# Copying the first batch's state five steps later in the first 256-token block of a fused retention and gated feed-forward kernel

## The chip, the cores and the metric

The kernel runs on one core of one Trainium2 chip. The metric is the device time of one execution in microseconds (us), taken as the median of several runs. Time before: 303.86 us, the median of three runs (303.48 to 303.89).

The engines are named as in the profile: PE is TensorE (matrix products), DVE is VectorE, ACT is ScalarE, POOL is GpSimd, and SP is the engine whose queue issues nearly all transfers.

## The reference

Retention (attention with a decay per head) on 8 batches, 8 heads, 576 positions and 64 elements per head, and then a gated feed-forward network on the 4608 tokens with 512 features and 1536 hidden units:

```python
scores = scale * np.matmul(q, k.transpose(0, 1, 3, 2))
gamma = 1.0 - 2.0 ** (-5.0 - np.arange(H))
rel = pos[:, None] - pos[None, :]
Dmat = np.where(rel >= 0, gamma[:, None, None] ** rel[None], 0.0)
attn = np.matmul(scores * Dmat[None], v)
x = attn.transpose(0, 2, 1, 3).reshape(B * S, H * D)
gate = 1.0 / (1.0 + np.exp(-(x @ w_gate)))
out = (gate * (x @ w_val)) @ w_out
```

## The kernel before

The positions of a batch are cut into chunks of 128 (the last one has 64). Inside a chunk the products of queries and keys are masked and multiplied with the values; what lies in earlier chunks enters through a running **state** per batch and head, a 64 x 64 matrix that sums key-by-value products. A last chunk of 64 positions needs the state after the fourth chunk.

The tokens pass in blocks: 512 tokens first, then the blocks of `BLOCKS`: two of 256 tokens (`w` = 0 and 1) and seven of 512. The first 512 tokens include the first batch's four whole chunks. That is why the first batch's state after its fourth chunk is already there, in the tile `sbd[3]`, before block 0 begins. `sbd[3]` holds it in block-diagonal form (two heads on each 128 x 128 square). The first batch's last chunk is handled much later, as step `(0, LAST)`, and it reads the state from a tile `sf` of the ordinary form. `first_batch_state()` (L833 to L840) makes that tile. It issues two copies on DVE for the halves that stay on their partitions, and two transfers from on-chip memory to on-chip memory on SP's queue for the halves that change partitions.

All instructions are in an order written out by hand. Each engine works through its own list in that order and waits on semaphores; nothing is rescheduled. In block `w` the generator `ffn_units` yields after each unit of PE work, and the list `SUMS_AT` says what is issued behind which unit: `0.3:w10v` means "in block 0, behind unit 3, issue weight sum number 0 of the value weights, group 1, on DVE" (the last letter is v for DVE, p for POOL; it has no effect for the letters c, t and f). The letters are: c `casts_to` (load, scale and cast the next chunks, mostly POOL and SP), f `first_batch_state`, g and w `w_sums` (sums of gate and value weights, L365), t `turn_step` (PE transposes a chunk, and ACT and DVE copy it out, L632), o `wo_sums` (L324).

The units of a 256-token block come from `h_units` (L876 to L891). Even units are the gate products of two hidden slices (PE `h_g`, then a sigmoid on ACT, L888); odd units are the value products (PE `h_v`, then the gate-times-value product on DVE, L890, with `gv` as output). The accumulators of the units turn through a ring of three PSUM banks, `ffn_psum`:

```python
ps = ffn_psum.tile([P, 2, n], FP32, tag="ffn", name=f"h_{what}_{t0}_{fc}")
...
if what == "g":
    nc.scalar.activation(out=both, in_=ps, func=AF.Sigmoid)
else:
    nc.vector.tensor_tensor(out=both, in0=both, in1=ps, op=ALU.mult)
```

Unit n + 3 takes the bank of unit n. Unit 4 (`h_g` of slices 4 and 5) may start when the DVE product of unit 1 has read its bank. Unit 9 is the value unit of slices 8 and 9, and unit 10 (`h_g` of slices 10 and 11) takes the bank of unit 7, so it waits for unit 7's DVE product. In the text a value unit's DVE product has its unit's number: "product 1" is L890 behind unit 1.

In block 0 the list reads: behind unit 0 the casts up to chunk step 3 and, before the change, the first batch's state; behind unit 3 three weight sums (`g20p` on POOL, `w10v` and `w11v` on DVE); behind unit 6 the turn of chunk step 1 (`t01p`); behind unit 7 `o10p`; behind unit 8 and 9 more; behind unit 10 the scores of two chunk steps (PE `row` and `new`).

Of the kernel before, what the change touches and what calls it, by code (L numbers as in the profile page):

```python
# [16 lines left out]
def kernel(  # L17
# [1477 lines left out]
    def op_first(fcs, nbs, opps):  # L1495
        for fc in fcs:
            for nb in nbs:
# [49 lines left out]
    store(opps[3], 3 * P, on_act)  # L1547
    casts_to(1)

    SUMS_AT = ("0.0:c03p 0.0:f00p 0.3:g20p 0.3:w10v 0.3:w11v 0.6:t01p 0.7:o10p 0.8:c02v "  # L1550
# [4 lines left out]
    sums_at = {}  # L1555
    for x in SUMS_AT:
        at, x = x.split(":")
# [87 lines left out]
```

## Time and profile before

| what | before |
|---|---|
| median of three runs | 303.86 us |
| the profiled execution: its time | 303.85 us |
| its span in the trace | 302.0 us |
| PE busy | 295.0 us (98%) |
| DVE busy | 228.5 us (76%) |
| POOL busy | 222.8 us (74%) |
| ACT busy | 204.5 us (68%) |
| granted PE clock | full in all 40 slices |

The span runs from the first to the last recorded instruction; 1.85 us of the profiled execution's time lie outside of it. A row of the timeline has the start in us, the duration in us, the engine, the line, the operation, output and inputs, and how many instructions were merged; in brackets stands the idle time of the engine before it, and what ended that. Start times count from the start of the span. PE's matrix products are pipelined, so a row's duration reaches into the next row.

### The profile page before, as it was taken

Reading aid. Unit: us, or ns where it says so; the run is one execution under the profiler, and the core shown is the slowest. Engines: PE = TensorE matmul, PEld = TensorE weight load, DVE = VectorE, ACT = ScalarE, POOL = GpSimd, SP = SyncE. Lnnn points to the kernel's source line nnn. Section 1 sums busy time; section 2 is a strip of 40 time slices with the busy share of each in tenths; the row PEclk is TensorE's granted clock in tenths of the full one; section 3 lists DMA queues with packets and bytes.
Section 4 is the critical chain, followed back from the end, with each engine's and each line's share of the span. In section 5 each row is a group of like instructions: output and inputs, shape, how many; then the busy total and the mean of one; then the engine's idle time right before and its main releaser. Section 6 shows DMA issues by size and latency. Waiting matters only on the chain.

```text
span 302.0 us, 10687 instructions
## 1 busy us (share of the span) xinstructions
PE 295.0 (98%) x4430; PEld 249.8 (83%) x4437; DVE 228.5 (76%) x433; ACT 204.5 (68%) x413; POOL 222.8 (74%) x250
## 2 busy tenths in 40 slices
PE   7999999999999999999999999999999999999994
PEld 3687786878868888888888888888888888888883
DVE  6968666875887998789748974896489948945893
ACT  6765464335359747985798589857985698559830
POOL 5675545936569888978997899689978946860780
PEclk9999999999999999999999999999999999999999
DMA  7999999998989989998649967966694154004013
GB/s 200 339 365 401 346 311 245 233 144 186 188 177 212 247 161 209 218 203 243 143 106 207 249 144 156 239 166 141 116 203 141 37 148 168 4 2 140 3 35 104
DMA packets 146464, 54.99 MB, mean 182 GB/s; under 512 B 124400, under 2 KB 139760, under 8 KB 146416
## 3 DMA queue, kind: packets, MB, share of 16 engines
q1 hardware_dynamic: 145328, 53.59, 74.3%
q10 hardware_dynamic: 1088, 0.72, 0.8%
q8 instruction: 34, 0.56, 0.7%
q14 instruction: 14, 0.11, 0.1%
HBM read 37.75 MB, written 9.44 MB: 156 GB/s over the span
## 4 chain that ended last, share of the span: by engine, by line
PE 94%; SPq 2%; DMA 2%; DVE 1%; issue 0%; POOL 0%
PE gatea L1015 12%; PE wa L1015 12%; PE qa L1142 11%; PE qe L1142 9%; PE gatee L1015 6%; PE we L1015 6%; PE h_g L885 4%; PE op L1275 3%; PE op L1502 3%; PE h_v L885 3%; PE gateg L1015 3%; PE wg L1015 3%; PE hg L1343 3%; PE hv L1343 3%; SPq L186 2%; PE val L717 2%
## 5 line engine op out<-in xcount | busy, mean ns | idle before, releaser
L1015 PEld LDWEIGHTS <-wg_sb 128*128 128x128 bf16 x336 | 32.9, 98 | 4.0
L1042 POOL TENSOR_TENSOR gv<-gv,wu 128x512 bf16<-128x512 bf16 x20 | 23.4, 1172 | 15.8 <-DVE wu L1054 15.7
L1142 PEld LDWEIGHTS <-gsum 128*128 128x128 bf16 x312 | 29.9, 98 | 3.7
L429 POOL TENSOR_TENSOR qk<-q,qtab 128x512 bf16<-128x512 f32 x28 | 30.2, 1079 | 3.4 <-DMA q<-in_q_dram 3.4
L1015 PEld LDWEIGHTS <-wv_sb 128*128 128x128 bf16 x296 | 28.9, 98 | 3.4
L1054 DVE TENSOR_TENSOR gu<-gatee,gu 128x512 f32<-128x512 f32 x21 | 14.5, 691 | 19.1 <-ACT gateg L1046 10.1
L942 POOL TENSOR_TENSOR gsum<-gsum,gv 128x256 bf16<-128x256 bf16 (+1 forms) x20 | 17.6, 890 | 14.4 <-DVE gsum L942 12.6
L1015 PEld LDWEIGHTS <-wgt_sb 128*128 128x128 bf16 x252 | 24.6, 98 | 2.9
L1015 PE MATMUL gatea<-xsum,wg_sb 128*128 128x256 bf16 x168 | 25.0, 273 | 0.0
L1142 PEld LDWEIGHTS <-gv 128*128 128x128 bf16 x228 | 21.8, 98 | 2.7
L942 POOL TENSOR_TENSOR gsum<-gv,gsum 128x256 bf16<-128x256 bf16 (+1 forms) x24 | 21.9, 920 | 0.2
L703 DVE TENSOR_TENSOR pt<-row,tri 128x512 bf16<-128x512 f32 x30 | 19.3, 682 | 3.4 <-PE row L686 3.0
L1057 DVE TENSOR_TENSOR gs<-gatea,gs 128x512 f32<-128x512 f32 x21 | 14.5, 689 | 9.3 <-PE gatea L1015 9.2
L429 POOL TENSOR_TENSOR qk<-k,ktab 128x512 bf16<-128x512 f32 x11 | 11.5, 1042 | 13.5 <-DMA k<-in_k_dram 6.2
L442 POOL TENSOR_TENSOR v<-v,ktab 128x512 bf16<-128x512 f32 x19 | 20.9, 1100 | 0.0
L1015 PE MATMUL wa<-xsum,wv_sb 128*128 128x256 bf16 x136 | 20.4, 273 | 0.0
L658 ACT CAST sb<-s 128x512 bf16<-128x512 f32 (+1 forms) x26 | 14.4, 568 | 8.3 <-DVE s L828 8.2
L787 ACT CAST xT<-val 128x512 bf16<-128x512 f32 x26 | 14.7, 592 | 6.8 <-PE val L733 6.8
L942 DVE TENSOR_TENSOR gsum<-gv 128x512 bf16<-128x512 bf16 (+1 forms) x34 | 18.7, 577 | 0.0
L1015 PEld LDWEIGHTS <-wvt 128*128 128x128 bf16 x168 | 16.4, 98 | 1.9
L942 POOL TENSOR_TENSOR gsum<-gv 128x256 bf16<-128x256 bf16 (+1 forms) x20 | 17.5, 879 | 0.0
L1042 POOL TENSOR_TENSOR gv<-gv,ws 128x512 bf16<-128x512 bf16 x14 | 16.3, 1162 | 1.0 <-DVE ws L1057 1.0
(203 smaller groups left out, 878.2 us busy)
## 6 DMA issues: line engine op xcount, KB each, us to landing
k<-in_k_dram SPq DMA_DIRECT2D x26, 256.0 KB, 3.9
q<-in_q_dram SPq DMA_DIRECT2D x26, 256.0 KB, 4.3
v<-in_v_dram SPq DMA_DIRECT2D x26, 256.0 KB, 4.5
out_dram<-ob SPq DMA_DIRECT2D x24, 256.0 KB, 3.3
wg<-in_moe_w_gate_dram SPq DMA_DIRECT2D x12, 256.0 KB, 5.3
wv<-in_moe_w_val_dram SPq DMA_DIRECT2D x12, 256.0 KB, 5.2
wo<-in_moe_w_out_dram SPq DMA_DIRECT2D x12, 256.0 KB, 5.1
v32p<-in_v_dram SPq DMA_DIRECT2D x6, 256.0 KB, 4.8
```

The costliest lines, as they stand in the source:

```text
L429: eng.tensor_tensor(out=to, in0=by_halves(loaded[s][1 - i]), in1=tab, op=ALU.mult)
L442: nc.gpsimd.tensor_tensor(out=natural["v", s], in0=loaded[s][2], in1=tab, op=ALU.mult)
L703: nc.vector.tensor_tensor(out=t[:, y, 0:n].rearrange("p i m t -> p (i m) t"), in0=rows_tile[ss[0]][y][:, 0:n].rearrange("p i m t -> p (i m ...
L787: nc.scalar.copy(out=to, in_=src)
L885: nc.tensor.matmul(ps[:, i], lhsT=w_sb[:, kc, (fc + i) * P:(fc + i + 1) * P], rhs=xT(kc, slice(t0, t0 + n)), start=(kc == 0), stop=(kc == ...
L942: eng.tensor_tensor(out=to, in0=a, in1=b, op=op)
L1015: nc.tensor.matmul(ps[:, f], lhsT=w[:, kc, f * P:(f + 1) * P], rhs=x[:, kc], start=(first and f == 0 and kc == 0), stop=(f == 1 and kc == ...
L1042: eng.tensor_tensor(out=to, in0=to, in1=src[:, part], op=ALU.mult)
L1054: nc.vector.tensor_tensor(out=me["u2"], in0=e, in1=me["u2"], op=ALU.add)
L1057: nc.vector.tensor_tensor(out=me["s5"], in0=a, in1=me["s5"], op=ALU.add)
L1142: nc.tensor.matmul(ps[:, b], lhsT=left(fp)[:, b * P:(b + 1) * P], rhs=right(fp), start=(first and fp == 0 and b == 0), stop=(fp == NFC // ...
L1343: nc.tensor.matmul(ps[:, cols], lhsT=(wg_sb if what == "g" else wv_sb)[:, kc, fc * P:(fc + 1) * P], rhs=xT(kc, cols), start=(kc == 0), sto ...
```

## The change

One entry of `SUMS_AT` gets another place: `first_batch_state()` is issued behind unit 5 of block 0 and no longer behind unit 0. What it issues stays the same.

```diff
-    SUMS_AT = ("0.0:c03p 0.0:f00p 0.3:g20p 0.3:w10v 0.3:w11v 0.6:t01p 0.7:o10p 0.8:c02v "
+    SUMS_AT = ("0.0:c03p 0.5:f00p 0.3:g20p 0.3:w10v 0.3:w11v 0.6:t01p 0.7:o10p 0.8:c02v "
```

In DVE's list the two copies stood ahead of products 1 and 3, the two weight sums and product 5; now they stand behind these five, and ahead of the copy of the turned chunk (L632) and product 7. In SP's list the two transfers keep their place, between the transposing transfers of chunk steps 3 and 4. The lists of PE, ACT and POOL keep their order.

## The prediction

> **What bounds the kernel now.** I read the page's busy shares and its chain first, then the list of what PE waited for, then the chain in order of time around the edit, and last the timeline of each engine there.
>
> ```profile
> PE 295.0 (98%) x4430; PEld 249.8 (83%) x4437; DVE 228.5 (76%) x433; ACT 204.5 (68%) x413; POOL 222.8 (74%) x250
> PE 94%; SPq 2%; DMA 2%; DVE 1%; issue 0%; POOL 0%
> ```
>
> PE is the bound: 94% of the chain that ended last is PE work. A change of DVE's order counts only where PE waits. PE's waits over the whole span are few:
>
> ```profile
> PE idle L242 <- DVE blank L229: 1.1, 1, 1.1
> PE qkp L485 <- ACT qT L476: 0.6, 2, 0.4
> PE h_g L885 <- DVE gv L890: 0.5, 1, 0.5
> ```
>
> The third lies at the edit. The chain in order of time (start, us, what) shows the copies in it:
>
> ```profile
> 53.15 0.89 PE h_g L885 x8
> 54.03 0.63 DVE sf L838
> ...
> 54.70 0.70 DVE gv L890
> 55.40 0.04 issue
> 55.44 1.03 PE h_g L885 x8
> ```
>
> Unit 4 (the `h_g` at 55.44) needs product 1, which stands on DVE behind the copies. Here are the rows of PE, then DVE, then POOL, and the copies apart (min/median/max in ns).
>
> ```profile
> 52.11 1.04 PE L885 MATMUL h_v<-xT,wv_sb 128*128 128x256 bf16 x8
> ...
> 53.85 1.04 PE L885 MATMUL h_v<-xT,wv_sb 128*128 128x256 bf16 x8
> 55.44 1.03 PE L885 MATMUL h_g<-xT,wg_sb 128*128 128x256 bf16 x8 [0.55 <-DVE gv L890]
> 56.31 1.04 PE L885 MATMUL h_v<-xT,wv_sb 128*128 128x256 bf16 x8
> ...
> 58.50 1.04 PE L885 MATMUL h_v<-xT,wv_sb 128*128 128x256 bf16 x8
> ...
> 61.12 1.04 PE L885 MATMUL h_g<-xT,wg_sb 128*128 128x256 bf16 x8
> ```
>
> ```profile
> 52.98 1.68 DVE L838 COPY sf<-sbd 64x128 bf16<-64x128 bf16 x2
> 54.70 1.28 DVE L890 TENSOR_TENSOR gv<-gv,h_v 128x512 bf16<-128x512 bf16 x2
> 55.90 1.30 DVE L365 TENSOR_TENSOR wvt<-wv_sb 128x512 bf16<-128x512 bf16 x1
> 57.23 0.71 DVE L365 TENSOR_TENSOR wvt<-wvt,wv_sb 128x512 bf16<-128x512 bf16 x1
> 57.87 0.68 DVE L890 TENSOR_TENSOR gv<-gv,h_v 128x512 bf16<-128x512 bf16 x1
> 58.70 0.42 DVE L632 COPY T<-turn 128x512 bf16<-128x512 bf16 x1 [0.16 <-PE turn L630]
> 59.65 0.69 DVE L890 TENSOR_TENSOR gv<-gv,h_v 128x512 bf16<-128x512 bf16 x1 [0.52 <-PE h_v L885]
> ```
>
> ```profile
> L838 DVE COPY sf<-sbd x2: 644/834/1024, 53.0 to 54.0; 64x128 bf16<-64x128 bf16 x2
> ```
>
> ```profile
> 52.47 1.49 POOL L429 TENSOR_TENSOR qk<-q,qtab 128x512 bf16<-128x512 f32 x1
> 54.01 0.61 POOL L444 CAST v<-v 128x512 bf16<-128x512 f32 x1
> 54.87 1.04 POOL L429 TENSOR_TENSOR qk<-k,ktab 128x512 bf16<-128x512 f32 x1 [0.26 <-DMA k<-in_k_dram]
> 55.87 1.04 POOL L429 TENSOR_TENSOR qk<-q,qtab 128x512 bf16<-128x512 f32 x1
> 56.86 0.81 POOL L444 CAST v<-v 128x512 bf16<-128x512 f32 x1
> 57.63 1.33 POOL L365 TENSOR_TENSOR wgt_sb<-wg_sb 128x512 bf16<-128x512 bf16 x1
> 58.92 1.15 POOL L324 TENSOR_TENSOR wt_sb<-wo_sb 128x512 bf16<-128x512 bf16 x1
> ```
>
> The copies are small (64 partitions, 128 elements each), yet take 1.68 us. Laid beside POOL's rows, the reason shows. Copy 1 lasts 1.02 us, from 52.98 to 54.00, and POOL's product ends at 52.47 + 1.49 = 53.96. Copy 2 ends at 52.98 + 1.68 = 54.66, and POOL's cast ends at 54.01 + 0.61 = 54.62. Each copy ends 0.04 us after the POOL instruction that was running when it came. **So a copy waits until the running POOL instruction ends, and needs next to nothing itself.** The weight sums behave alike: `w10` ends at 57.20, 0.28 us after POOL's product (56.91); `w11` at 57.94, 0.28 after POOL's cast (57.67). In both cases POOL's next instruction had been issued (0.04 us before the last one's end), and DVE still got its turn in between; POOL paid for that with 0.20 us (cast 0.81 against 0.61) and 0.18 us (1.33 against 1.15). The products L890 and the turned copy L632 read PSUM and keep 0.68 and 0.42 us beside a busy POOL: they wait for nobody.
>
> The Trainium skill states this as a lock: "SBUF — State Buffer", section "Who interferes with whom", says that DVE and GpSimd share one port pair, that a DVE copy in a two-port mode, or a DVE operation with two inputs on chip, takes it for its whole duration, and that whoever issues first blocks the other fully. The same section exempts a DVE operation with one on-chip input outside of those modes; by that exemption the copies would be free and the sum would be that of the first rival below. This trace has the two copies waiting, 1.02 and 0.64 us.
>
> **The change, part by part.**
>
> *The wait that goes.* Unit 3 starts on PE at 53.85 and its matmuls take 0.87 us of PE's time (the next `h_v` to `h_g` distances, as 55.44 to 56.31), so unit 4 could start at 54.72. It starts at 55.44. Without the copies product 1 waits for unit 1 alone: that ends at 52.11 + 1.04 = 53.15, DVE follows 0.11 later (unit 7: 58.50 + 1.04 = 59.54, product at 59.65), and 0.69 us later, at 53.95, the bank is free, 0.77 before 54.72. **Gain: 0.71 us**, more than the 0.55 of the wait's row, since the pipeline also refills.
>
> *DVE's list up to the new place.* Product 3 starts at 53.85 + 1.04 + 0.11 = 55.00 and ends at 55.69. `w10` is issued 0.08 before that (as 55.90 before 55.98), at 55.61, during POOL's product of k (54.87 to 55.91). It ends at 55.91 + 0.28 = 56.19. POOL's product of q is held up by 0.19 and ends at 57.10. `w11`, issued at 56.22, meets it and ends at 57.10 + 0.28 = 57.38; POOL's cast ends near 57.86. Product 5 runs from 57.30 to 57.98. Unit 8 stands two units of 0.87 ahead of unit 10 (61.12), so it needs that only at 59.38 − 0.71 = 58.67.
>
> *The copies in the new place.* Copy 1 is issued at 57.90, 0.08 before product 5's end. POOL issued its weight sum `g20` 0.04 before the cast's end, at 57.82. So POOL comes first, by 0.04 to 0.08 us, and copy 1 waits for a whole 1.15 us: to 57.82 + 1.15 = 58.97, done at 59.01. POOL's `o10`, issued by then, goes next; copy 2, issued at 59.02, waits for it to the end, 1.15 later, and is done at 60.20. The pattern (copy 1 behind one POOL instruction, copy 2 behind the next) is the one of before, with two longer instructions.
>
> *What is queued behind.* The turned copy takes 60.23 to 60.65, product 7 from 60.58 to 61.26. Before, product 7 ended at 59.65 + 0.69 = 60.34, with time to spare. Unit 10 takes its bank; it would start at 61.12 − 0.71 = 60.41, and now starts 0.05 after product 7 (as 55.44 after 55.40), at 61.31. **A new wait of 0.90 us.** The turned copy's reader (`row`, behind unit 10) is not reached before that.
>
> *SP and the readers.* The two transfers keep their place:
>
> ```profile
> 58.64 1.69 SPq L448 DMA_TRANSPOSE T<-qk  x1
> 60.38 1.39 SPq L838 DMA_DIRECT2D sf<-sbd  x2
> 62.09 1.27 SPq L448 DMA_TRANSPOSE T<-qk  x1
> L733 PE MATMUL val<-T,sf x64: 186/193/211, 109.3 to 267.0; 64*64 64x64 bf16 x64
> ```
>
> They run at 60.38 behind the transpose of 58.64, later than either place of the copies, and PE reads no `sf` tile before 109.3: cover of nearly 50 us, cost nothing.
>
> *The sum.* −0.71 + 0.90 = +0.19 us. The profiled execution takes 303.85 us, 0.01 under the median: 303.85 + 0.19 = **304.04 us**. PE has no wait behind 55.44, so the shift reaches the end as it is. A measurement of this kernel tells about 0.2% (0.61 us) from no change; +0.19 is within that. Bounds of the unknown: a copy that needn't wait costs some 0.05 us (it ends 0.04 after POOL), and at most one whole POOL instruction of 1.15, so the two cost 0.1 to 2.3 us. I take 2.3, by the order of issue, though that order hangs on 0.04 to 0.08 us.
>
> **The rivals.**
>
> *At most one copy is blocked.* If copy 1 slips in ahead of `g20`, copy 2 ends near 59.0, product 7 near 60.1, and unit 10 has its bank in time. PE keeps 0.71 there. But the next rows show little slack on another path:
>
> ```profile
> 62.00 0.42 DVE L324 TENSOR_TENSOR wt_sb<-wo_sb 128x512 bf16<-128x512 bf16 x1
> 62.60 1.29 DVE L703 TENSOR_TENSOR pt<-row,tri 128x512 bf16<-128x512 f32 x2 [0.18 <-PE row L686]
> 65.39 1.07 ACT L658 CAST sb<-s 128x512 bf16<-128x512 f32 x2 [2.60 <-DVE s L828]
> 66.65 0.24 PE L733 MATMUL val<-T,sb 64*64 64x64 bf16 x8
> 61.03 1.04 POOL L429 TENSOR_TENSOR qk<-q,qtab 128x512 bf16<-128x512 f32 x1
> ```
>
> `o00` on DVE (62.00) would be issued near 61.3, meet POOL's product (to 62.07) and end near 62.35, as before (62.42); the masks behind it (62.60) move up only 0.3, and so does the cast that ends at 65.39 + 1.07 = 66.46, 0.2 before PE uses it. PE can move up 0.5: 303.35 us. For it speaks how narrow copy 1's race is; against it, that copy 2 of before was blocked by a cast issued at 54.01, just ahead of it (52.98 + 1.02 = 54.00 is copy 1's end). Chance 0.17. That neither copy waits, since nothing holds a copy back but some other cause that the old place had, gives the same 303.35 by the same slack; chance 0.03, as both old copies end so exactly behind POOL's rows. The exemption in the Trainium skill named above would lead to this case.
>
> *The whole gain stays.* As above, with the masks less tied than I read them: 303.85 − 0.71 = 303.14 us, 0.23% faster. Chance 0.08.
>
> *Slower.* POOL's sequence hangs on one landing: the k of 54.87 (0.26 of waiting). All later steps above follow its end at 55.91. If k lands later, `w10`, both POOL sums, the copies and unit 10 go with it, us for us, while the gain of 0.71 stays fixed. From 0.42 us later on the kernel is slower by over 0.2%; the limit is 55.61, where `w10` would come first: +0.19 + 0.74, or 304.78 us. Against it: SP's order is the same, so k should land as before. Chance 0.12, with other losses behind the new wait.
>
> **How the numbers follow.** The forecast has 0.60. Most of the first rival's spread (303.2 to 303.6) counts as within 0.2%, and the forecast's own spread is 303.7 to 304.5 as k lands 0.3 earlier or later. The range 303.25 to 304.55 leaves out the whole gain and most of the slower case, somewhat under 0.2. Faster: 0.08 and a quarter of the first rival's 0.20, 0.13. Slower: 0.12 and a tail of the forecast, 0.15. Same: 0.72.
>
> **What would show it.** Right: unit 4 at 54.72 with no wait; two copies from about 57.9 to 60.2, each ending 0.04 after a POOL row (`g20`, `o10`); a PE wait of some 0.8 us before unit 10, the `h_g` near 61.3, ended by DVE `gv`. Wrong: copies under 0.2 us, or no PE wait there (first two rivals); the k product on POOL well past 54.87 (slower); unit 4 still waiting (the gain's reading fails).

## The result and the profile after

The changed kernel takes 305.00 us (median of 22 runs, 303.19 to 307.80); the kernel before, beside it on the same chip, 303.88 us (22 runs, 303.07 to 305.19). The ratio is 1.0032 (1.0018 to 1.0045): slower by about 1 us, where 304.04 us was forecast. Three later comparisons of the same pair on other chips gave 1.000 (0.997 to 1.003), 1.000 (0.998 to 1.002) and 1.0004 (0.998 to 1.0027); four single runs on a further one took 304.67 to 307.27 against 303.98 (one run). So the loss is resolved on the first chip and on none of the later three comparisons. The traces below show two courses of the changed kernel in block 0; which one a run takes is decided by whether POOL's product of k starts before DVE issues `w10`. How much of the median of 305.00 us comes of that is not shown.

The profiled execution of the changed kernel took 304.06 us (span 302.2), one of its shorter runs. Its page and PE's waits:

```profile
PE 295.5 (98%) x4437; PEld 250.1 (83%) x4437; DVE 228.9 (76%) x433; ACT 204.1 (68%) x413; POOL 223.3 (74%) x250
PE 95%; DMA 2%; ACT 1%; POOL 0%; SPq 0%; issue 0%; DVE 0%
```

```profile
PE idle L242 <- DVE blank L229: 1.1, 1, 1.1
PE kTp L466 <- POOL kp L412: 0.6, 1, 0.6
```

The wait of `h_g` on `gv` is gone, and no new one stands in its place; the wait that is new (`kTp`, 0.6 us) lies at the start, before the edit. PE, DVE and POOL around block 0, in this trace:

```profile
51.92 1.04 PE L885 MATMUL h_g<-xT,wg_sb 128*128 128x256 bf16 x8
...
54.54 1.04 PE L885 MATMUL h_v<-xT,wv_sb 128*128 128x256 bf16 x8
55.42 1.04 PE L885 MATMUL h_g<-xT,wg_sb 128*128 128x256 bf16 x8
...
61.10 1.04 PE L885 MATMUL h_g<-xT,wg_sb 128*128 128x256 bf16 x8
62.07 0.45 PE L686 MATMUL row<-T 64*64 64x64 bf16 x32
```

```profile
56.29 0.55 DVE L365 TENSOR_TENSOR wvt<-wv_sb 128x512 bf16<-128x512 bf16 x1
56.88 1.15 DVE L365 TENSOR_TENSOR wvt<-wvt,wv_sb 128x512 bf16<-128x512 bf16 x1
57.95 0.67 DVE L890 TENSOR_TENSOR gv<-gv,h_v 128x512 bf16<-128x512 bf16 x1
58.55 0.98 DVE L838 COPY sf<-sbd 64x128 bf16<-64x128 bf16 x2
59.57 0.43 DVE L632 COPY T<-turn 128x512 bf16<-128x512 bf16 x1
60.02 0.69 DVE L890 TENSOR_TENSOR gv<-gv,h_v 128x512 bf16<-128x512 bf16 x1
```

```profile
55.96 0.61 POOL L444 CAST v<-v 128x512 bf16<-128x512 f32 x1 [1.43 <-DMA v<-in_v_dram]
56.63 1.12 POOL L429 TENSOR_TENSOR qk<-k,ktab 128x512 bf16<-128x512 f32 x1
57.71 1.22 POOL L429 TENSOR_TENSOR qk<-q,qtab 128x512 bf16<-128x512 f32 x1
58.88 0.61 POOL L444 CAST v<-v 128x512 bf16<-128x512 f32 x1
```

Unit 4 follows unit 3 without a gap (54.54, 55.42). Each copy again ends 0.04 to 0.05 us behind a POOL row: copy 1 behind the product of q (57.71 + 1.22 = 58.93), copy 2 behind the cast (58.88 + 0.61 = 59.49, copies' end 59.53). But these are not the two rows that the forecast named. POOL waited 1.43 us for a load of v, so its product of k began at 56.63, after DVE had issued `w10` (56.29). `w10` passed it, the weight sums met POOL rows that stand one place earlier in POOL's list than forecast, the copies two places earlier, and the copies took 0.98 us instead of 2.3. Product 7 ends at 60.71, 0.39 before unit 10.

From unit 0 to `row` this takes 62.07 − 51.92 = 10.15 us. The same two rows of PE in the first trace of before:

```profile
51.23 1.04 PE L885 MATMUL h_g<-xT,wg_sb 128*128 128x256 bf16 x8
...
62.09 0.44 PE L686 MATMUL row<-T 64*64 64x64 bf16 x32
```

That was 10.85 us by the unrounded starts, so the block gained 0.70 us. The execution was longer by 0.21 us all the same: unit 0 began 0.69 later, and from `row` to the end it took 0.23 longer (241.99 against 241.76, counted to the execution's time). Neither explains a median 1 us longer, so this one trace could not settle the case.

### The profile page after: what moved, and what is told of

Same layout as the page of the kernel before. It is cut to its first block, busy times and chain, and to the rows that moved or that the text cites. A ratio compares the mean times of both kernels' runs of the same rounds, so it can differ in the third digit from the quotient of the medians.

```text
span 302.2 us, 10694 instructions
## 1 busy us (share of the span) xinstructions
PE 295.5 (98%) x4437; PEld 250.1 (83%) x4437; DVE 228.9 (76%) x433; ACT 204.1 (68%) x413; POOL 223.3 (74%) x250
## 4 chain that ended last, share of the span: by engine, by line
PE 95%; DMA 2%; ACT 1%; POOL 0%; SPq 0%; issue 0%; DVE 0%
PE gatea L1015 12%; PE wa L1015 12%; PE qa L1142 11%; PE qe L1142 9%; PE gatee L1015 6%; PE we L1015 6%; PE h_v L885 4%; PE op L1502 4%; PE op L1275 4%; PE h_g L885 3%; PE gateg L1015 3%; PE wg L1015 3%; PE hg L1343 3%; PE hv L1343 3%; PE val L717 2%; PE qa L1218 2%
```

## The experiments

**The changed kernel again, and the copies taken off DVE or elsewhere.** `act5` and `act0` do the two copies on ACT, behind unit 5 and behind unit 0; `late10` puts the DVE copies into block 1.

```diff
-                (nc.vector.tensor_copy if hh == y else nc.sync.dma_start)(
+                (nc.scalar.copy if hh == y else nc.sync.dma_start)(
```

```diff
-    SUMS_AT = ("0.0:c03p 0.5:f00p 0.3:g20p 0.3:w10v 0.3:w11v 0.6:t01p 0.7:o10p 0.8:c02v "
-               "0.9:o00v 0.11:c05p 0.11:c07p 0.12:w13v 0.12:c06v 0.14:g21v 0.14:g23p 1.0:o20v "
+    SUMS_AT = ("0.0:c03p 0.3:g20p 0.3:w10v 0.3:w11v 0.6:t01p 0.7:o10p 0.8:c02v "
+               "0.9:o00v 0.11:c05p 0.11:c07p 0.12:w13v 0.12:c06v 0.14:g21v 0.14:g23p 1.0:f00p 1.0:o20v "
```

> The changed kernel once more, for a second trace: the first trace has no PE wait before unit 10 and took 304.06 us, a us under the median of 305.0. Theory L (lock): the two copies in the new place wait for POOL in most runs, product 7 comes late and unit 10 waits; the trace of a run near 305 shows a PE wait on DVE gv of 1 to 2 us there. Theory E (elsewhere): block 0 gains its 0.5 to 0.7 us in each run, and the loss of some 1.1 us lies before or behind it; then the trace shows no wait before unit 10 though the time is near 305.

> The two copies stand in the new place (behind unit 5) but are done by ACT, so they use no VectorE port and nothing on DVE is behind them. Theory L: no wait before unit 4 and none before unit 10: 303.1 to 303.5 us, 1.5 us under the changed kernel. Theory E: the loss stays, 304.5 to 305 us.

> The two copies stand in the old place (behind unit 0) but are done by ACT. Theory L: the old wait of 0.71 us before unit 4 is gone and no new one comes: 303.1 to 303.5 us. Theory E says that taking the copies out from ahead of products 1 and 3 is itself what loses: 304.5 to 305 us.

> The copies stay on DVE and move to block 1, behind its unit 0, where DVE idles 1.56 us before product 1; the two transfers move behind the loads and transposes of chunk steps 4 to 7 on SP. Theory L: 303.1 to 303.5 us. Theory E: 304.5 to 305 us, since block 0 without the copies ahead of products 1 and 3 is the same as in the changed kernel.

| kernel | median, runs | against before (304.36 us) | unit 0 to `row` in its trace |
|---|---|---|---|
| after_again | 304.53, 12 | 1.000 (0.997 to 1.003) | 10.15 |
| act5 | 304.19, 12 | 0.9988 (0.996 to 1.0016) | 10.15 |
| act0 | 304.82, 12 | 1.0008 (0.9978 to 1.0038) | 10.15 |
| late10 | 304.43, 12 | 1.0005 (0.9973 to 1.0038) | 10.15 |

Neither theory's times came: none of the three is 1 us faster, and none is resolved from before. The trace of `after_again` went theory E's way: a run of 305.04 us with no wait before unit 10, where theory L had expected one of 1 to 2 us. The runs of one kernel spread over 2 to 4 us, and the traces say why times decide little here: unit 0 itself begins anywhere from 51.23 to 52.51 us in these four and the first trace of before, which lies ahead of every edit here. The stretch from unit 0 to `row` is free of that. In the three variants without copies ahead of product 1 or 7 it is 10.15 us, and in `after_again`, whose copies took 0.98 us, as well. A copy that is not held up is short, on DVE (the second one in `late10`) and on ACT:

```profile
L838 DVE COPY sf<-sbd x2: 192/295/398, 70.2 to 70.6; 64x128 bf16<-64x128 bf16 x2
L838 ACT COPY sf<-sbd x2: 285/289/293, 56.9 to 57.2; 64x128 bf16<-64x128 bf16 x2
```

(192 ns is the second copy in block 1, with POOL idle; the first, 398 ns, ended behind a POOL row. In `before_c` and `dbl0` copies that met an idle POOL took 0.19 us too. The forecast had "some 0.05 us" for a copy that needn't wait, which is too low. Of a copy's 0.19 us 0.05 is left when POOL's row ends, and of `w10`'s 0.42 unhindered 0.28 is left; so an estimate from these rows is that some 0.14 us of either has passed before it is held.)

**The copies doubled, and before and after once more.** `dbl0` and `dbl5` issue the pair of DVE copies twice, in the old and in the new place.

```diff
+        for hh in range(2):
+            nc.vector.tensor_copy(out=whole[half(hh), hh::2, :], in_=sbd[3][half(hh), 2 * hh:2 * hh + 2, half(hh)])
```

> The kernel before once more, for a second trace. In the first trace POOL's product of k started 0.14 us behind the place that unit 4 would have without its wait; in the five other traces, of other kernels, it started 0.6 to 2.0 us behind unit 4. Theory P (phase): POOL and its loads stand elsewhere against PE in each run, and the 0.71 us wait before unit 4 belongs to runs with an early POOL; a trace with POOL 0.6 us or more behind shows a wait of 0 to 0.3 us. Theory S (steady): the wait is 0.5 to 0.8 us in any run.

> The changed kernel, a third trace, and its ratio once more. Theory P: the copies end behind two POOL instructions, no wait before unit 10 where POOL is 0.9 us or more behind unit 4, and a wait up to 0.9 us where it is earlier; ratio 1.000 to 1.004. Theory S, with the gain of 0.7 us in each run: ratio 0.998.

> The kernel before with the two DVE copies issued twice in the old place (the second pair writes the same data again). Theory P: each further copy waits for a POOL instruction or passes in 0.2 us, so 0.4 to 2 us more on DVE, and unit 4 starts as much later: 304.4 to 305.5 where the kernel before has 303.9 to 304.4. If PE's waits behind the block take up any shift (theory E), within 0.2 us of the kernel before.

> The changed kernel with the two DVE copies issued twice in the new place. Theory P: 1 to 2 us more on DVE ahead of product 7, which has 0.3 to 0.4 us to spare in the two traces of the changed kernel: a PE wait of 0.5 to 1.7 us before unit 10, and 0.5 to 1.7 us above the changed kernel. Theory E: within 0.2 us of the changed kernel.

`after_b`: 1.000 (0.998 to 1.002), 304.02 us, with seven runs from 303.46 to 304.11 and five from 305.00 to 305.73, none between; its trace had k 0.90 us behind unit 4 and no wait, as theory P said. `dbl0`: 1.0027 (1.0003 to 1.005), 305.09 us, in theory P's range; but in its one trace (304.05 us) the second pair met an idle POOL, took 0.41 us, and the block took 10.69 us, so what made the median longer is not in that trace. `dbl5`: 1.0131 (1.0081 to 1.018), 308.03 us of 6 runs, three at 305.92 to 306.54 and three at 309.52 to 309.98; even the lower three are further above the changed kernel than theory P had expected. In its trace, a run of 306.00 us, the first pair took 0.98 us as in the changed kernel; the second pair met the two weight sums, and unit 10 waited:

```profile
58.84 2.19 DVE L840 COPY sf<-sbd 64x128 bf16<-64x128 bf16 x2
61.06 0.42 DVE L632 COPY T<-turn 128x512 bf16<-128x512 bf16 x1
62.26 1.03 PE L887 MATMUL h_g<-xT,wg_sb 128*128 128x256 bf16 x8 [1.58 <-DVE gv L892]
```

So in these traces the second pair cost 1.74 us of the block in the new place (11.89 against 10.15) and nothing in the old one (10.69, and 10.68 in `before_b`). Theory E of these runs, that waits behind the block take up any shift, falls with `dbl5`; that other losses lie outside the block is not excluded by it. In `before_b` (304.08 us) the old wait was there, but smaller:

```profile
55.66 1.03 PE L885 MATMUL h_g<-xT,wg_sb 128*128 128x256 bf16 x8 [0.38 <-DVE gv L890]
```

POOL's product of k was early here too (55.32, 0.20 us behind unit 4's undisturbed start), so this trace does not separate theories P and S.

**Is it PE's earliness, or the copies?** `pad5` gives PE 0.65 us of idle work in the place of the old wait (six matmuls whose result is overwritten).

```diff
+                if t0 == BLOCKS[0][0] and fc == 4 and what == "g":
+                    for _ in range(6):
+                        nc.tensor.matmul(ps[:, 0], lhsT=w_sb[:, 0, fc * P:(fc + 1) * P], rhs=xT(0, slice(t0, t0 + n)),
+                                         start=True, stop=True)
```

> The changed kernel: so far its runs fall into two groups, near 303.8 and near 305.2 us, 24 of 46 above 304.9, against 13 of 86 of the kernel before. Its three traces show no wait before unit 4 and none before unit 10. Theory G: without the 0.7 us wait before unit 4 PE stands closer to the loads and POOL behind the block, and in about half of the runs something there loses 1 to 1.5 us; again 4 to 8 of 12 runs above 304.9. Theory C (the copies behind unit 5): in half of the runs the copies meet the two weight sums and unit 10 waits a us. Both give ratio 1.000 to 1.004.

> The copies behind unit 5, on ACT. Theory G: as the changed kernel, about half of the runs above 304.9. Theory C: nothing on DVE stands ahead of product 7, so few runs (0 to 3 of 12) above 304.9 and a median of 303.6 to 304.2 us, under the kernel before.

> The changed kernel with six matmuls of unit 4's first product issued once more ahead of unit 4 (they are overwritten): 0.65 us of PE time in the place of the old wait. Theory G: PE stands behind the loads as in the kernel before, so the group near 305.2 is gone again (0 to 3 of 12 above 304.9), median 303.9 to 304.3. Theory C: the copies stand as in the changed kernel against POOL, product 7 has 0.65 us more, so few runs above 304.9 as well, but then act5 has few too. If neither holds, the whole distribution is that of the changed kernel plus 0.65 us.

> The kernel before, a third trace beside these: a wait of 0.4 to 0.7 us before unit 4 and no other one above 0.3 us behind it, whatever POOL's place.

`after_c`: 1.0004 (0.998 to 1.0027), 304.58 us, 5 of 12 above 304.9, which both theories allow; its trace, of the shortest run, had no wait before unit 10. `act5_b`: 1.0017 (0.9989 to 1.0044), 305.03 us, 7 of 12 above 304.9, against theory C: its copies are on ACT and its block took 10.15 us, and yet it has as many long runs. But on this chip the kernel before had a median of 304.71 and 10 of 29 runs above 304.9, so that such counts tell little here. `pad5`: 1.0014 (0.9996 to 1.0033), 305.32 us, 9 of 12 above 304.9, so theory G's cure does not work; what fits is the third outcome on record, the changed kernel plus 0.65 us (305.32 − 304.58 = 0.74). Its trace was the first to show the forecast's course in full: k was ahead of `w10` by 0.13 us, `w10` took 1.19 us, both copies ended behind the two weight sums, and unit 10 waited:

```profile
58.62 2.22 DVE L838 COPY sf<-sbd 64x128 bf16<-64x128 bf16 x2
62.07 1.03 PE L889 MATMUL h_g<-xT,wg_sb 128*128 128x256 bf16 x8 [0.72 <-DVE gv L894]
```

`before_c` (303.62 us) went against its expectation, and against the forecast: no wait before unit 4 at all. The copies took 1.23 us there, the second one with POOL idle, but product 1 was done in time:

```profile
52.73 1.23 DVE L838 COPY sf<-sbd 64x128 bf16<-64x128 bf16 x2
53.98 1.04 PE L885 MATMUL h_v<-xT,wv_sb 128*128 128x256 bf16 x8
54.85 1.04 PE L885 MATMUL h_g<-xT,wg_sb 128*128 128x256 bf16 x8
```

**Four more traces of the changed kernel, to see its long runs.**

> The changed kernel, one look. Theory P (phase): if POOL's product of k starts before DVE issues w10, then w10 takes about 1.2 us or its own wait, the two copies take 2.2 us together and end with POOL's g20 and o10, unit 10 waits 0.9 to 1.6 us, unit 0 to row takes 11.0 to 11.8 us; if it starts after w10, the copies take 0.98 us, there is no wait and unit 0 to row takes 10.15 us. Theory E (elsewhere): unit 0 to row is 10.15 us in any run, and long runs lose behind the block.

> As after_d. Theory P: 11.0 to 11.8 us from unit 0 to row if k is ahead of w10, else 10.15. Theory E: 10.15 in any case.

> As after_d. Theory P: 11.0 to 11.8 us from unit 0 to row if k is ahead of w10, else 10.15. Theory E: 10.15 in any case.

> As after_d. Theory P: 11.0 to 11.8 us from unit 0 to row if k is ahead of w10, else 10.15. Theory E: 10.15 in any case.

All traces of the two kernels, and those of two variants on the first later chip, in us ("k ahead" is how long POOL's product of k began before DVE issued `w10`):

| trace | time | k ahead | `w10` took | the two copies | unit 0 to `row` |
|---|---|---|---|---|---|
| before | 303.85 | 1.03 | 1.30 | 1.02 + 0.64 | 10.85 |
| before_b | 304.08 | 0.80 | 0.52 | 1.03 + 0.54 | 10.68 |
| before_c | 303.62 | −0.75 | 0.79 | 1.03 + 0.19 | 10.15 |
| after | 304.06 | −0.34 | 0.55 | 0.43 + 0.54 | 10.15 |
| after_again | 305.04 | −0.08 | 0.42 | 0.43 + 0.54 | 10.15 |
| after_b | 303.93 | −0.02 | 0.42 | 0.43 + 0.54 | 10.15 |
| after_c | 303.45 | −0.56 | 0.76 | 0.43 + 0.54 | 10.15 |
| after_d | 304.67 | −0.24 | 0.42 | 0.43 + 0.59 | 10.15 |
| after_e | 305.95 | −0.85 | 0.42 | 0.37 + 0.99 | 10.15 |
| **after_f** | 305.29 | **0.10** | 1.23 | **1.11 + 1.10** | **11.71** |
| **after_g** | 307.27 | **0.09** | 1.24 | **1.11 + 1.11** | **11.73** |
| act5 (copies on ACT) | 304.37 | 0.29 | 1.04 | none on DVE | 10.15 |
| late10 (copies later) | 304.57 | 0.25 | 1.07 | none in block 0 | 10.15 |

The rule of theory P, put on record ahead of `after_d` to `after_g`, holds in these four and fits the four traces before them; only the copies of `after_e` took 1.37 us in place of 0.98, behind two earlier POOL rows and without a wait on PE. Where k is ahead of `w10`, by as little as 0.09 us, the block takes 1.56 to 1.58 us longer; where it isn't, by as little as 0.02 us, it takes 10.15. The two nearest, `after_b` and then `after_g`:

```profile
56.34 0.42 DVE L365 TENSOR_TENSOR wvt<-wv_sb 128x512 bf16<-128x512 bf16 x1
56.37 1.30 POOL L429 TENSOR_TENSOR qk<-k,ktab 128x512 bf16<-128x512 f32 x1 [0.26 <-DMA k<-in_k_dram]
```

```profile
57.21 1.04 POOL L429 TENSOR_TENSOR qk<-k,ktab 128x512 bf16<-128x512 f32 x1 [1.50 <-DMA k<-in_k_dram]
57.30 1.24 DVE L365 TENSOR_TENSOR wvt<-wv_sb 128x512 bf16<-128x512 bf16 x1
```

The variants `act5` and `late10` are the control: k is ahead there too, `w10` is held up (1.04 and 1.07 us), but with no copies ahead of product 7 nothing comes of it. `after_f` in detail, first PE, then DVE, then POOL:

```profile
51.65 1.04 PE L885 MATMUL h_g<-xT,wg_sb 128*128 128x256 bf16 x8
...
55.14 1.04 PE L885 MATMUL h_g<-xT,wg_sb 128*128 128x256 bf16 x8
...
62.40 1.03 PE L885 MATMUL h_g<-xT,wg_sb 128*128 128x256 bf16 x8 [1.41 <-DVE gv L890]
63.36 0.45 PE L686 MATMUL row<-T 64*64 64x64 bf16 x32
```

```profile
56.02 1.23 DVE L365 TENSOR_TENSOR wvt<-wv_sb 128x512 bf16<-128x512 bf16 x1
57.28 1.15 DVE L365 TENSOR_TENSOR wvt<-wvt,wv_sb 128x512 bf16<-128x512 bf16 x1
58.35 0.68 DVE L890 TENSOR_TENSOR gv<-gv,h_v 128x512 bf16<-128x512 bf16 x1
58.95 2.22 DVE L838 COPY sf<-sbd 64x128 bf16<-64x128 bf16 x2
61.20 0.42 DVE L632 COPY T<-turn 128x512 bf16<-128x512 bf16 x1
61.66 1.28 DVE L890 TENSOR_TENSOR gv<-gv,h_v 128x512 bf16<-128x512 bf16 x2
```

```profile
55.92 1.04 POOL L429 TENSOR_TENSOR qk<-k,ktab 128x512 bf16<-128x512 f32 x1 [1.55 <-DMA k<-in_k_dram]
56.92 1.22 POOL L429 TENSOR_TENSOR qk<-q,qtab 128x512 bf16<-128x512 f32 x1
58.10 0.80 POOL L444 CAST v<-v 128x512 bf16<-128x512 f32 x1
58.87 1.14 POOL L365 TENSOR_TENSOR wgt_sb<-wg_sb 128x512 bf16<-128x512 bf16 x1
59.97 1.15 POOL L324 TENSOR_TENSOR wt_sb<-wo_sb 128x512 bf16<-128x512 bf16 x1
```

The race is lost by 0.08 us, as forecast: POOL issues `g20` at 58.87, copy 1 comes at 58.95 and ends at 60.06, 0.05 behind `g20` (58.87 + 1.14 = 60.01); copy 2 ends at 58.95 + 2.22 = 61.17, 0.05 behind `o10` (59.97 + 1.15 = 61.12). Then the turned copy, product 7, and unit 10 at 62.40.

A long time alone doesn't tell the course. `after_e` and `after_again` are long with a block of 10.15 us. Beside `after_b` (303.93 us), unit 0 began 1.10 us later in `after_e` and 0.36 in `after_again`, and from `row` to the end they took 0.91 and 0.74 longer. PE's longest waits in them, besides the first one of every trace, lie ahead of the block:

```profile
PE hv L1343 <- ACT share L532: 1.6, 1, 1.6
```

```profile
PE hg L1343 <- ACT gv L1347: 0.7, 1, 0.7
```

Over the eight traces of the changed kernel unit 0 begins at 51.15 to 53.08 us, and the stretch behind `row` takes 241.81 to 242.72. In the three of before it is 51.23 to 51.63 and 241.76 to 242.12. So what lies outside the block moves a run by as much as the two courses do.

That the long course makes the median of 305.00 is therefore argued and not shown: of the 22 runs one alone has a trace, and it took the short course. For it speaks that `after_f` stands 1.36 us above `after_b`'s trace (305.29, 303.93), and `after_b`'s upper group of runs some 1.6 above its lower one; and that on the first chip 14 of 22 runs lie above 304.9 us, against 1 of 22 of before. Against it speaks `act5_b`, whose median of 305.03 came with the copies on ACT and 10.15 us in its traced block, though on a chip where before had 304.71. Why k is late in more runs on one chip than on another stays open.

## Why the prediction was wrong

- **The chain of holds.** Right, row by row: in `after_f` and `after_g` the copies wait for `g20` and `o10`, take 2.2 us (2.3 forecast), delay the turned copy and product 7, and unit 10 waits. But this happened in two of the changed kernel's eight traces; in the other six the copies took 0.98 to 1.37 us and no wait came.
- **The size of the new wait, the term that was mis-sized.** Forecast 0.90 us; measured 11.71 − 10.15 = 1.56 us in the block. It hangs on k's place, as the slower rival said: "us for us". The forecast put the start of k's product 0.14 us behind unit 4's undisturbed start (54.87 against 54.72, or 54.73 by unrounded starts). In `after_f` it is 0.78 behind (55.92 against 55.14), 0.64 more; 0.90 + 0.64 = 1.54.
- **The step that failed.** "SP's order is the same, so k should land as before", with which the slower rival got 0.12, and in the range "as k lands 0.3 earlier or later". The order is the same, the place of POOL's product of k is not: over the traces of all variants it begins between 0.14 and 2.0 us behind unit 4's undisturbed start, and the trace of before was the earliest of all. Nor is it one landing: POOL waited at k itself in `after_f` and `after_g` (1.55 and 1.50 us), at the cast of v in front of it in `after` and `after_c` (1.43 and 1.56). The forecast took one draw for a fixed place. In the block the slower rival's mechanism, its price and its limit were right: by it the loss ends where k is 55.61 − 54.72 = 0.89 behind unit 4, and 0.79 (`after_g`) was long, 0.90 (`after_b`) short. But the median of 305.00 us lies above its 304.78, and how the 1.1 us between the medians divides between the block and the rest stays open.
- **"The shift reaches the end as it is."** In `after` 0.70 us were gained in the block, and the run was longer by 0.21. What lies outside the block moves by tenths to 1.9 us from run to run, so a shift of this size can't be followed to the end in single runs; whether the edit has a part in the longer stretches behind the block, three traces of before can't tell.
- **The gain of 0.71 us.** Also a draw: 0.70, 0.53 and 0.00 us in the three traces of before (10.85, 10.68, 10.15 against 10.15). In `before_c`, where POOL came late, the old place cost nothing, and there was nothing to win.
- **The first rival** (at most one copy blocked) had the right outcome for the short course by another way: both copies wait, but for the rest of a product and for a cast of 0.61 us, since `w10` slipped past k. The tie behind it shows in `after` and `after_c`, where `o00` took 1.02 and 1.22 us. From `row` to the PE product L1275 behind the second `row` it took 5.54 and 5.74 us there, against 5.47 in the first trace of before: a loss of 0.07 and 0.27, where the rival had 0.2.
- **The lock.** The Trainium skill ("SBUF — State Buffer", section "Who interferes with whom") says that the shared port pair is held for a whole instruction, and that whoever issues first blocks the other. The rows agree in both directions: in `after_b` `w10` comes first and takes 0.42 us, and POOL's product 1.30 in place of 1.04; in `after_g` the product comes first and takes 1.04, and `w10` 1.24. A difference of 0.02 to 0.10 us in who comes first turns 1.56 us.
- **The sum.** By the traces, the block gains 0 to 0.70 or loses 0.86 to 1.58 us. The forecast's +0.19 was one pair of draws, and its range, built on one landing, ended at 304.55.

None of the variants is a version that measurably beats both kernels: `act5` has the undisturbed 10.15 us in both of its traces, but 0.9988 and 1.0017, with intervals that hold 1.

## What to carry to other kernels

Where an instruction's cost is a wait for another engine's running instruction, its price in one trace is a draw: find what sets the two engines against each other (here the place of POOL's list, behind its loads), and price the edit over the whole spread of it, not at the one place seen. A wait of half a microsecond in a single trace can be absent in the next one of the same kernel, as here before unit 4. A small copy is safest where nothing that PE will soon need stands behind it on its engine, since its wait lasts as long as whatever the other engine is doing.

## What the runs showed of the hardware

A race of hundredths of a microsecond between DVE and POOL was passed on through four holds and came out as 1.56 us on PE: `after_b` (k 0.02 us behind `w10`, 10.15 us) and `after_g` (0.09 ahead, 11.73 us) lie on the two sides of the turning point. In `dbl5`, three runs at 305.92 to 306.54 us had a granted clock of 1.000, and three at 309.52 to 309.98 one of 0.992 to 0.994; one run of `dbl0` (307.98 us, 0.994) and one of `act5_b` (308.12 us, 0.993) had such a clock too. None of the runs at the lower clock has a trace, so whether a longer wait lowers the clock, or both come from something else, stays open.
